# Coarser loads, deeper buffers and a new hand-written order in a sketched-attention kernel with a gated convolution

## The chip, the core and the metric

The kernel runs on one core of a Trainium2 chip. The core has five engines that run their own instruction lists in order and meet through semaphores: TensorE (PE), VectorE (DVE), ScalarE (ACT), GpSimd (POOL) and SyncE (SP, which here only issues DMAs). ACT can issue DMAs too. The metric is the device time of one execution in microseconds (us), as a median over runs.

## What is computed

For each of 4 batches and 4 heads, q, k and v are 1088 tokens of 32 numbers. A sketch phi maps a token to 64 numbers, the outer product of two projections to 8. Keys and values are summed into one 64x32 matrix per head (linear attention without a mask), each query is read against it and divided by its denominator. The heads are joined to 128 channels; a causal depthwise convolution of 5 taps gives a sigmoid gate, which multiplies a 128x128 product, and a second 128x128 product gives the output.

```python
def phi(x):
    a = np.einsum('rd,bhsd->bhsr', S1, x); b = np.einsum('rd,bhsd->bhsr', S2, x)
    return np.einsum('bhsi,bhsj->bhsij', a, b).reshape(*x.shape[:-1], r * r)
q_p, k_p = phi(q), phi(k)
kv = np.einsum('bhsf,bhsd->bhfd', k_p, v); z = np.sum(k_p, axis=2)
num = np.einsum('bhsf,bhfd->bhsd', q_p, kv)
den = np.einsum('bhsf,bhf->bhs', q_p, z)[..., None] + 1e-06
x = (num / den).transpose(0, 2, 1, 3).reshape(B, S, H * D)
gate = sigmoid(sum(conv_w[t] * xp[:, t:t + S, :] for t in range(5)))   # xp: x with 4 zeros in front
out = (gate * (x @ w_val)) @ w_out
```

## The kernel before

A batch lies in SBUF as 128 rows: 4 heads by 32 blocks m, with 34 tokens t in a row. Every piece of work is a small step function (`s_kt`, `s_kp` and so on), and the string `ORDER` lists all steps by hand: `kt20` is step kt of batch 2, part 0, and the digits behind a colon say which of seven PSUM banks it uses. Nothing else orders the work: each engine runs its share of the list in that order and holds everything behind an instruction that waits.

The steps of one batch, with the engine that does each:

- `ld`: DMA loads on SP, constants and weights on ACT. k and q of batch 0 come in two parts, of the other batches whole (544 KB); v comes as four loads of 128 KB by j (8 tokens of each row for 32 partitions) and two of 16 KB for the last two tokens (`v_lo`).
- K side: `kt` transposes k on DVE, `kp` projects on PE, `ke` copies to `kab` on ACT, `kd` (DVE) and `ko` (POOL) form the outer products `phik` (the table `KD` says how many chunks DVE takes), `kv` sums them against v on PE.
- `pz`, `pv`, `pm`, `pe`: the sums become weights for the query side (DVE, ACT, PE, ACT).
- Q side, in halves U and groups g: `qt` transposes q (DVE), `qp` projects (PE), `qc` copies (ACT), `qm`, `qr`, `qn` make the denominator, its sum and reciprocal (`qr`, DVE) and the scaled first factor `an` (DVE or POOL by `QM_POOL` and `QN_POOL`), `qo` the outer product `phi` (DVE or POOL by `QO_POOL`), `qx` transposes it on PE, `qe` copies it to `phiT` (ACT, or DVE where `ON_DVE` names it), `nm` is the numerator (PE) and `xe` copies it to the gate's input.
- Gate: `hl` copies the halo (POOL), `gt` is the convolution as 5 diagonal matmuls (PE), `sg` the sigmoid (ACT), `vl` the value product (PE), `gv` gate times value (DVE), `om` the output product (PE), `oe` the copy to SBUF, `so` the store (SP, or ACT by `ST_ACT`).
- `cn`: constants (masks and identities on POOL, wq on DVE, weight casts on POOL); `zz` and `cn06` are dummy matmuls on zeros. `cn10` in the order runs the mask step a second time.

Most tiles have two buffers by batch or half, `phi` and `phiT` three. A DMA uses one of eight completion semaphores in turn, and its issue waits until the DMA that last used this semaphore has landed. All matmuls but the transposes go through the helper `mm` and so stand under L138 in the profile; copies by ACT through `copy` under L220, by DVE under L218.

Of the kernel before, what the change touches and what calls it, by code (L numbers as in the profile page):

```python
# [9 lines left out]
BF16 = mybir.dt.bfloat16  # L10
AX = mybir.AxisListType
# [13 lines left out]


ORDER = """
cn08 ld00 cn00 ld02 cn06:01 ld03 ld06 cn09 cn10 cn01 cn07 ld07
cn02 kt00 zz07:2 ld12 ld04 kt01 ld05 ld16 kp00:2 kp01:3 ke00 zz04:0
kd00 ko00 ke01 ld01 ko01 ld17 kd01 kv00 zz01:0 ld22 kv01 ld14  # L30
kt10 ld26 zz03:0 pv00 pz00 qt00 kp10:4 pm00:5 qt01 ke10 kp11:6 pe00
ld27 ko10 kd10 qp00:0 ke11 ld32 kd11 ko11 qp01:1 ld24 qc00 ld36
kv10 qm00 qc01 cn05 qr00 kv11 qm01 qn00 qr01 cn03:2 zz02:3 pv10
qo01 cn04 pz10 qo00 ld37 pm10:3 kt20 qx00:5 ld34 qn01 qx01:4 pe10
qo02 qe00 qo03 kp20:6 qe01 nm00:0 qt10 qx02:2 ke20 qx03:3 nm01:5 qe02
kp21:1 ko20 qe03 nm02:4 kd20 qp10:2 ke21 xe01 kd21 ko21 xe02 qp11:3
qc10 xe00 nm03:6 kv20 qm10 qc11 qr10 hl00 xe03 kv21 qm11 qn10
qr11 gt00:54 qo11 pv20 pz20 kt30 vl00:1 pm20:0 sg00 sg01 gt01:26 pe20
qn11 gv00 kp30:5 qo10 qt20 sg03 sg02 kp31:4 ke30 vl02:0 ko30 qx10:1
qo12 ke31 vl03:6 qp20:2 qe10 ko31 gv02 kd31 gv03 nm10:4 qx12:3 kd30  # L40
qc20 om01:0 qx11:1 xe10 qp21:6 oe01 qm20 qr20 qe12 kv30 so02 qo13
so03 qt30 kv31 qe11 qn20 qc21 qx13:4 pz30 qo20 nm11:5 qo21 pv30
nm12:0 qe13 vl01:3 pm30:1 xe11 nm13:6 gv01 qm21 qx21:4 xe12 qx20:2 pe30
hl10 qr21 om00:50 qe21 qp30:3 xe13 qn21 qe20 oe00 qo22 nm21:1 gt11:46
qc30 xe21 so00 vl12:2 qm30 qo23 nm20:0 sg12 vl13:5 qr30 qx22:1 so01
xe20 qp31:4 sg13 gv12 qe22 qn30 qx23:0 gv13 gt10:62 qc31 qo30 qo31
qe23 nm22:1 qm31 sg10 vl11:5 qr31 vl10:3 nm23:0 sg11 om11:4 qx30:6 xe23
hl20 gv10 qx31:2 oe11 qn31 gv11 gt20:03 qe30 qo33 xe22 so12 qe31
om10:45 sg20 so13 vl20:1 nm30:6 sg21 qo32 qx33:0 gv20 xe30 nm31:2 vl21:3
oe10 qe33 gt21:16 gv21 xe31 so10 nm33:0 sg22 qx32:4 hl30 om20:52 xe33  # L50
sg23 so11 vl22:3 qe32 vl23:1 gt30:60 oe20 gv22 nm32:4 so20 gv23 sg30
vl31:2 vl30:5 xe32 sg31 om21:3 so21 gv30 gt31:16 oe21 gv31 vl32:4 om30:05
sg32 so22 vl33:3 sg33 gv32 oe30 so23 gv33 om31:2 so30 so31 oe31
so32 so33
# [4 lines left out]
def kernel(  # L59
# [34 lines left out]
    v_in = [st(f"v_in{b}", [P, H, 8 * D]) for b in range(B)]  # L94
    v_lo = [st(f"v_lo{b}", [64, H, D]) for b in range(B)]
    kT = [st(f"kT{i}", [P, NT * M]) for i in range(2)]
    qT = [st(f"qT{i}", [P, NT, M]) for i in range(2)]
    kab = [st(f"kab{i}", [P, 2, 5, 32]) for i in range(2)]
    phik = [st(f"phik{i}", [P, 5, H, 64]) for i in range(2)]
    zm = [st(f"zm{i}", [P, 32]) for i in range(2)]  # L100
    kvf = [st(f"kvf{i}", [P, 2, 64]) for i in range(2)]
    kvb = [st(f"kvb{i}", [P, P], BF16) for i in range(2)]
    wq = [st(f"wq{i}", [P, 96]) for i in range(2)]
    abc = [st(f"abc{i}", [P, 3, 5 * 32]) for i in range(2)]
    pden = [st(f"pden{i}", [P, 20, 9]) for i in range(2)]
    den = [st(f"den{i}", [P, 20]) for i in range(2)]
    an = [st(f"an{i}", [P, 20, 8]) for i in range(2)]
    phi = [st(f"phi{i}", [P, 12, 64], BF16) for i in range(3)]
    phiT = [st(f"phiT{i}", [P, 2, 320], BF16) for i in range(3)]
    xe = [st(f"xe{i}", [P, 4 + NT, M], BF16) for i in range(2)]  # L110
    gate = [st(f"gate{i}", [P, 320], BF16) for i in range(4)]
    gv = [st(f"gv{i}", [P, 576], BF16) for i in range(2)]
# [14 lines left out]
    wo_f = st("wo_f", [P, 2, P])  # L127
# [26 lines left out]
    def s_const(b, i):  # L154
# [13 lines left out]
        elif i == 9:  # L168
            make_identity(nc, ident32)
            make_identity(nc, ident)  # L170
            for t in range(2):
                nc.gpsimd.memset(pden[t], 1e-6)
                nc.gpsimd.memset(xe[t][:, 0:4, 0:1], 0.0)
                nc.gpsimd.memset(kvb[t], 0.0)
        elif i == 1:
            nc.vector.transpose(sT[:, 0, :], s1raw)
            nc.vector.transpose(sT[:, 1, :], s2raw)
            nc.vector.tensor_mul(
# [4 lines left out]
        elif i == 2:  # L183
            nc.vector.tensor_copy(out=wq[1][:, 0:64], in_=wq[0][:, 0:64])
# [7 lines left out]
            )  # L192
        elif i == 3:
# [7 lines left out]
        elif i == 5:  # L201
            nc.gpsimd.tensor_copy(out=wv, in_=wv_f)
            nc.gpsimd.tensor_copy(out=wo, in_=wo_f)
        elif i == 6:
            for t in range(9):
                mm(bank("cn", b, i, t % 2), zero[:, 0:P], zero)
        elif i == 7:
            nc.scalar.activation(out=gate[0][:, 0:1], in_=zero[:, 0:1], func=ACT.Sigmoid)
        elif i == 8:
            nc.vector.memset(zero, 0.0)  # L210
# [11 lines left out]
    def s_ld(b, i):  # L222
        if i == 0:
            nc.scalar.dma_start(out=s1raw, in_=bc(S1, 0, [16, r, D]))  # L224
            nc.scalar.dma_start(out=s2raw, in_=bc(S2, 0, [16, r, D]))
        elif i == 1:
# [306 lines left out]
```

## Time and profile before

| | us |
|---|---|
| timed runs | 58.89, 61.43, 59.87; median 59.87 |
| profiled execution, device time | 58.25 |
| its span | 56.2 |
| PE busy in the span | 46.1 (82%) |
| DVE busy | 37.5 (67%) |
| ACT busy | 32.7 (58%) |
| POOL busy | 31.8 (57%) |
| DMA: bytes moved, mean rate | 9.32 MB, 166 GB/s |

The span runs from the first to the last instruction of the profile; the device time has some 2 us around it. Busy time of PE counts matmuls from start to modelled end, so that a chain of dependent small matmuls looks full. A row of a group gives line, engine, operation, output and input tiles, shapes, count, then busy time, mean duration in ns, and the idle time of the engine just before. The slices cut the span in 40 parts of 1.4 us, one digit each in tenths. The chain of waits follows the work that ended last back to what released it.

### The profile page before, as it was taken

To read this page: it belongs to the slowest core of one execution; us is meant where nothing else is said; L and a number is where in the kernel's file an instruction comes from. 1 tells how busy PE (TensorE), PEld (TensorE's weight loads), DVE (VectorE), ACT (ScalarE), POOL (GpSimd) and SP (SyncE) were. 2 spreads that over 40 slices of the span, in tenths; PEclk is the share of its full clock that TensorE was granted. 3 is DMA by queue.
4 is the path that set the end of the run, shared out by engine and by line. 5 is a ranking of instruction groups with operands and counts; after the bars stand their busy time and mean duration, and the time that the engine had idled before them with its cause. 6 is when DMAs were issued, how large, how long until landed. Compare 5 with 4: busy or idle time off the path is not lost.

```text
span 56.2 us, 2707 instructions
## 1 busy us (share of the span) xinstructions
PE 46.1 (82%) x1131; PEld 34.0 (61%) x1131; DVE 37.5 (67%) x89; ACT 32.7 (58%) x90; POOL 31.8 (57%) x61
## 2 busy tenths in 40 slices
PE   1999989999999788999914999999999999972000
PEld 0334374758984486886804998888979776640000
DVE  1013948959898779888676889696899679850000
ACT  0450014015647999755830698799999997894000
POOL 4894008703679948979960599969799940000000
PEclk9999999999999999999999999999999999999955
DMA  0597999976679999999528302400331247566870
GB/s 0 146 332 208 183 308 381 249 127 146 116 248 421 274 222 323 317 275 169 106 44 251 142 0 47 146 18 12 89 77 44 55 96 184 137 156 156 216 213 0
DMA packets 7254, 9.32 MB, mean 166 GB/s; under 512 B 2245, under 2 KB 4938, under 8 KB 7242
## 3 DMA queue, kind: packets, MB, share of 16 engines
q1 hardware_dynamic: 6256, 8.52, 57.1%
q10 hardware_dynamic: 986, 0.63, 4.7%
q8 instruction: 9, 0.15, 1.2%
q14 instruction: 3, 0.02, 0.1%
HBM read 6.92 MB, written 2.23 MB: 163 GB/s over the span
## 4 chain that ended last, share of the span: by engine, by line
PE 44%; DMA 25%; DVE 8%; issue 6%; ACT 4%; ACTq 2%; SPq 1%; DVEq 0%
PE ring L138 33%; DMA q_in<-in_q_dram 11%; DMA wv_f<-in_moe_w_val_dram 8%; DMA s2raw<-in_S_dram 6%; PE ring L408 5%; PE kv L138 5%; DVE qT L340 2%; DVE kT L256 2%; ACTq L224 1%; ACT osb L220 1%; ACT phiT L220 1%; ACTq L479 1%; DVE xe L218 1%; SPq L235 1%; ACT kab L272 1%
## 5 line engine op out<-in xcount | busy, mean ns | idle before, releaser
L278 POOL TENSOR_TENSOR phik<-kab 128x256 f32<-128x256 f32 (+3 forms) x8 | 9.5, 1182 | 10.4 <-ACT kab L272 10.4
L394 POOL TENSOR_TENSOR phi<-an,abc 128x512 bf16<-128x512 f32 (+1 forms) x11 | 13.0, 1189 | 0.5
L138 PE MATMUL ring<-zero 128*128 128x512 bf16 x26 | 8.7, 482 | 1.3 <-DVE zero L210 1.3
L272 ACT COPY kab<-ring 128x256 f32<-128x256 f32 (+1 forms) x8 | 3.2, 402 | 8.6 <-PE ring L138 8.3
L138 PE MATMUL ring<-wq,kT 128*64 128x64 f32 x144 | 6.0, 226 | 2.6 <-issue 2.0
L220 ACT COPY phiT<-ring 128x512 bf16<-128x512 bf16 (+1 forms) x13 | 7.7, 617 | 0.3 <-ACT phiT L220 0.2
L138 PEld LDWEIGHTS ring<-wq,kT 128*64 128x64 f32 x144 | 5.0, 137 | 4.2 <-issue 2.1
L453 DVE TENSOR_TENSOR gv<-gate,ring 128x256 bf16<-128x256 bf16 x16 | 6.3, 434 | 1.7 <-PE ring L138 1.2
L138 PE MATMUL ring<-wq,qT 128*64 128x96 f32 x144 | 7.2, 248 | 0.2 <-DVE qT L340 0.2
L408 PE MATMUL ring<-ident,phi 128*64 128x128 bf16 (+1 forms) x144 | 6.7, 219 | 0.2 <-POOL phi L394 0.2
L138 PEld LDWEIGHTS ring<-wq,qT 128*64 128x64 f32 x144 | 6.2, 137 | 0.5 <-DVE qT L340 0.4
L138 PE MATMUL ring<-xe,diag 64*64 64x256 bf16 (+1 forms) x160 | 6.5, 280 | 0.1
L278 DVE TENSOR_TENSOR phik<-ring,kab 128x768 f32<-128x768 f32 (+1 forms) x7 | 5.7, 833 | 1.2 <-ACT kab L272 1.2
L442 ACT ACTIVATE gate<-ring 128x256 bf16<-128x256 f32 (+1 forms) x16 | 5.6, 399 | 1.1 <-PE ring L138 1.0
L340 DVE STREAM_TRANSPOSE qT<-q_in 128x1088 f32<-128x1088 f32 (+2 forms) x5 | 5.2, 1063 | 1.2 <-DMA q_in<-in_q_dram 1.2
L138 PEld LDWEIGHTS <-zero 128*128 128x128 bf16 x26 | 2.8, 119 | 5.2 <-issue 2.9
L408 PEld LDWEIGHTS <-phi 128*64 128x64 bf16 (+1 forms) x144 | 5.2, 109 | 1.0 <-POOL phi L394 0.3
L256 DVE STREAM_TRANSPOSE kT<-k_in 128x1024 f32<-128x1024 f32 (+1 forms) x5 | 5.0, 1020 | 0.3 <-DMA k_in<-in_k_dram 0.3
L138 PE MATMUL kv<-phik,v_in 128*32 128x64 f32 x256 | 5.2, 222 | 0.0
L138 PEld LDWEIGHTS kv<-phik,v_in 128*32 128x32 f32 x256 | 4.4, 110 | 1.1 <-DVE phik L278 0.4
L363 ACT COPY abc<-ring 128x480 f32<-128x480 f32 (+1 forms) x8 | 4.2, 519 | 1.4 <-PE ring L138 1.1
L138 PEld LDWEIGHTS <-diag 64*64 64x64 bf16 x160 | 4.2, 106 | 1.2 <-issue 0.4
(62 smaller groups left out, 75.5 us busy)
## 6 DMA issues: line engine op xcount, KB each, us to landing
v_in<-in_v_dram SPq DMA_DIRECT2D x16, 128.0 KB, 5.2
out_dram<-osb SPq DMA_DIRECT2D x13, 128.0 KB, 2.4
k_in<-in_k_dram SPq DMA_DIRECT2D x3, 544.0 KB, 4.5
q_in<-in_q_dram SPq DMA_DIRECT2D x3, 544.0 KB, 6.2
out_dram<-osb ACTq DMA_DIRECT2D x3, 128.0 KB, 2.6
k_in<-in_k_dram SPq DMA_DIRECT2D x1, 288.0 KB, 3.5
q_in<-in_q_dram SPq DMA_DIRECT2D x1, 288.0 KB, 5.0
k_in<-in_k_dram SPq DMA_DIRECT2D x1, 256.0 KB, 2.9
```

The costliest lines, as they stand in the source:

```text
L138: nc.tensor.matmul(o, lhsT=lhsT, rhs=rhs, start=start, stop=stop, skip_group_check=True, **kw)
L218: nc.vector.tensor_copy(out=out, in_=in_)
L220: nc.scalar.copy(out=out, in_=in_)
L256: nc.vector.transpose(o, i_)
L272: nc.scalar.copy(out=kab[u][:, :, 0 : 4 + u, :], in_=kab_view(b, u))
L278: eng.tensor_mul(phik[u][:, c0:c1].rearrange("p c h (i j) -> p (c h) i j", i=r), bc(a_, 3, [P, n, r, r]), bc(b_, 2, [P, n, r, r]),)
L340: nc.vector.transpose(flat(qT[b % 2][:, t0 : t0 + n, :]), q_in[b][:, t0 * D : (t0 + n) * D])
L363: nc.scalar.copy(out=abc[U][:, k0:3, 0 : 32 * ns], in_=bank("qp", b, U)[:, 32 * ns * k0 : 96 * ns].rearrange("p (k x) -> p k x", k=3 - k0),)
L394: (nc.gpsimd if pool else nc.vector).tensor_mul(phi[(4 * b + g) % 3][:, 0:n, :].rearrange("p c (i j) -> p c i j", i=r), bc(an[U][:, lo : l ...
L408: nc.tensor.transpose(o[64 * (h % 2) : 64 * (h % 2) + 64, h // 2, c * P : c * P + n], phi[(4 * b + g) % 3][:n, 4 * c + h, :], ident[:n, :n],)
L442: nc.scalar.activation(out=gate[g][:, 0:n], in_=bank("gt", b, g // 2, g % 2)[:, 0:n], func=ACT.Sigmoid)
L453: nc.vector.tensor_mul(o[:, 0:512].rearrange("p (c w m j) -> p w j c m", c=4, w=2, m=M)[:, w], view(gate[g]), view(vl))
```

## The change

It rewrites the loads, the depth of the buffers, the split of work between engines and the whole order. A short description speaks of 30 loads instead of 46; by the code it is 31 load DMAs instead of 41.

- v is loaded by j with the last tokens in it: four loads per batch, of 8, 8, 9 and 9 tokens (`KEYS`), and `v_lo` goes. k's transposes follow the same split. The fifth chunk of the K side now stands in partitions 64 to 127.
- w_out is loaded once; the two half-swapped copies are made by POOL in the cast. The weights are loaded by SP after k of batch 2, and not by ACT.
- k of a batch is loaded before q of the batch before it, as in the old order (there too k and q are whole from batch 1 on); s2raw and half of v of batch 0 are on SP, s1raw and two loads of v on ACT.
- `wq` is made by POOL (`cn013`, copies in `cn011`); the second run of the masks goes.
- `kab`, `phik`, `abc`, `phi`, `phiT` and `gv` have four buffers, `kT`, `qT` and `xe` three, and the small ones one per batch.
- From batch 1 on both halves' denominators are summed and inverted in one instruction each (`qr`, `qi`).
- `KD`, `QM_POOL`, `QN_POOL`, `QO_POOL` and `ON_DVE` move work; the last output bank goes to two banks and is copied in halves by DVE (`oe31`) and ACT (`oe33`).

```diff
+KEYS = [(0, 8), (8, 8), (16, 9), (25, 9)]
 ORDER = """
...
+cn08 ls00 cn00 lk00 cn06:01 ls01 cn07 lk01 cn05 lv00 lv03 lv01
+cn09 lk10 cn01 lv02 kt00 lq01 lq00 cn02 zz05:2 cn010 cn013 lv10
+kt01 cn011 lv12 lv11 kp00:2 lv13 kp01:3 ke00 zz05:0 kd00 ko00 ke01
+kd01 lk20 ko01 kv00 lw00 kt10 lw01 kv01 qt01 lw02 kp11:4 pv00
+lq10 pz00 qt00 pm00:5 lv20 ke11 kp10:6 pe00 lv22 kd11 ko11 ke10
+qp00:0 lv21 ko10 qp01:1 kd10 qc00 zz03:2 kt20 lv23 qm00 cn012 lk30
+cn03:2 kv10 lq20 qc01 qr00 cn04 lv30 qm01 kp20:3 qi00 qr01 lv32
+qn00 kp21:5 qi01 lv31 qo00 qo01 kv11 lv33 ke21 qt10 ke20 lq30
+zz01:0 qn01 qx01:4 pv10 pz10 qo02 qo03 qx00:6 pm10:2 qe01 qe00 qx03:0
+pe10 nm01:3 ko21 kt30 qx02:1 qe03 qp11:4 xe01 qe02 nm00:6 ko20 nm03:2
+qp10:0 kd20 kd21 xe03 qc11 kp31:3 xe00 qt20 qc10 gt00:12 ke31 qm11
+ko31 vl01:4 qm10 sg00 vl00:5 kv20 qr10 sg01 qi10 kv21 gv01 qn11
+gv00 qn10 nm02:6 pz20 pv20 kp30:1 qo12 qo10 xe02 pm20:2 ke30 kd31
+om00:45 pe20 qx10:6 ko30 qx12:0 oe02 oe00 qp21:3 qe10 so04 qe12 so00
...
+om21:6 so20 sg30 gv31 gt31:13 oe21 gv30 vl32:0 so22 sg32 om30:54 sg33
+vl33:6 so23 gv32 oe30 gv33 oe32 so30 so31 om31:21 oe31 oe33 so34
+so33 so32
 """.split()
...
+    v_in = st("v_in", [P, B * H, 9 * D])
+    kT = [st(f"kT{i}", [P, 9 * 4 * M]) for i in range(3)]
+    kab = [st(f"kab{i}", [P, 2, 5, 32]) for i in range(4)]
...
+    def s_lv(b, j):
+        t0, n = KEYS[j]
+        queue("lv", b, j).dma_start(
+            out=v_in[32 * j : 32 * j + 32, H * b : H * b + H, 0 : n * D],
+            in_=v[b].rearrange("h (m t) d -> m h (t d)", m=M)[:, :, t0 * D : (t0 + n) * D],
+        )
+    def s_kt(b, u):
+        o = kT[b % 3].rearrange("p (c j m) -> p j c m", c=9, m=M)
+        for x in (u,) if b == 0 else (0, 1):
+            t0, n = KEYS[2 * x]
+            nc.vector.transpose(
+                o[:, 2 * x : 2 * x + 2, 0:n],
+                k_in[b][:, t0 * D : (t0 + 2 * n) * D].rearrange("p (j c d) -> p j c d", j=2, d=D),
             )
...
     def s_qr(b, U):
-        n = 4 * (5 - U)
-        nc.vector.tensor_reduce(out=den[U][:, 0:n], in_=pden[U][:, 0:n, :], axis=AX.X, op=ALU.add)
-        nc.vector.reciprocal(den[U][:, 0:n], den[U][:, 0:n])
+        x = rows(U) if b == 0 else slice(0, 36)
+        nc.vector.tensor_reduce(out=den[b % 2][:, x], in_=pden[b % 2][:, x, :], axis=AX.X, op=ALU.add)
+    def s_qi(b, U):
+        x = rows(U) if b == 0 else slice(0, 36)
+        nc.vector.reciprocal(den[b % 2][:, x], den[b % 2][:, x])
...
+    def s_oe(b, i):
+        if i == 2:
+            copy("oe", b, i, osb_lo[b], bank("om", b, 0, 1)[0:64, 0:P])
+            return
+        U = i % 2
+        o = osb[2 * b + U].rearrange("p c e -> p (c e)")
+        if last(b, U):
+            copy("oe", b, i, o[:, 256 * (i // 2) : 256 * (i // 2) + 256], bank("om", b, U, i // 2)[:, 0:256])
+        else:
+            copy("oe", b, i, o, bank("om", b, U))
...
-    KD = [[3, 2], [3, 3], [2, 2], [3, 0]]
-    QM_POOL = {(1, 1), (2, 1)}
-    QN_POOL = {(0, 0), (0, 1), (1, 0), (1, 1), (2, 0), (2, 1), (3, 0), (3, 1)}
-    QO_POOL = {(0, 1), (0, 2), (1, 0), (1, 1), (1, 3), (2, 0), (2, 2), (2, 3), (3, 1), (3, 2), (3, 3)}
+    KD = [[2, 3], [2, 5], [0, 3], [1, 2]]
+    QM_POOL = {(0, 0), (0, 1), (1, 1), (3, 1)}
+    QN_POOL = {(0, 0), (0, 1), (1, 0), (1, 1), (2, 0), (3, 1)}
+    QO_POOL = {(0, 1), (0, 2), (1, 1), (1, 2), (1, 3), (2, 2), (2, 3), (3, 0), (3, 1), (3, 2), (3, 3)}
     ON_DVE = {
-        ('oe', 0, 0), ('qe', 3, 1), ('qe', 3, 2), ('qe', 3, 3), ('xe', 0, 0), ('xe', 1, 3),
-        ('xe', 2, 2), ('xe', 3, 2), ('xe', 3, 3),
+        ('oe', 0, 2), ('oe', 1, 2), ('oe', 2, 2), ('oe', 3, 1), ('oe', 3, 2), ('qe', 0, 0),
+        ('qe', 1, 0), ('qe', 1, 2), ('qe', 2, 1), ('qe', 2, 2), ('qe', 2, 3), ('qe', 3, 0),
+        ('qe', 3, 1), ('qe', 3, 2), ('qe', 3, 3), ('xe', 1, 3), ('xe', 3, 0), ('xe', 3, 2),
+        ('xe', 3, 3),
     }
-    ST_ACT = {(0, 3), (3, 0), (3, 2)}
+    ON_ACT = {
+        ('ls', 0, 0), ('lv', 0, 2), ('lv', 0, 3), ('so', 0, 0), ('so', 2, 4), ('so', 3, 0),
+        ('so', 3, 2), ('so', 3, 3),
+    }
```

## The prediction

> **What bounds the kernel now.** I read the page's slices first, then the windows of seven microseconds, the chain of waits, and last the timeline around the chain's breaks. Slices (each 1.4 us):
>
> ```profile
> PE   1999989999999788999914999999999999972000
> ...
> DMA  0597999976679999999528302400331247566870
> GB/s 0 146 332 208 183 308 381 249 127 146 116 248 421 274 222 323 317 275 169 106 44 251 142 0 47 146 18 12 89 77 44 55 96 184 137 156 156 216 213 0
> ```
>
> Until 29 us loads and compute run side by side, later there are only stores. The DMA row is near full, yet bytes per slice fall from 381 to 116 GB/s between 11 and 15 us and to 44 at 28 us: the queue is held up there. PE has one dip, at 28 to 30 us. The chain of waits names both:
>
> ```profile
> 9.42 4.29 DMA wv_f<-in_moe_w_val_dram
> 13.71 0.02 issue
> 13.73 0.31 SPq L247
> ...
> 14.08 0.43 SPq L235
> ...
> 14.56 6.20 DMA q_in<-in_q_dram
> ...
> 28.31 1.99 issue
> ```
>
> A load of v's last tokens (L247) could not be issued before the weight wv had landed, and k and q of the next batches stood behind it on SP. The 1.99 us at 28.31 lie inside kp31, in the middle of one row of like matmuls: PE waits there for nothing that the profile shows. The windows give the late stage (us, then busy and count of PE, PEld, DVE, ACT, POOL):
>
> ```profile
> 35.00:42.00 7.00, 6.95 (x167) 5.77 (x165) 5.64 (x18) 6.51 (x19) 5.95 (x9) 1.00 0.28 70
> 42.00:49.00 7.00, 6.94 (x178) 5.41 (x176) 5.84 (x19) 6.57 (x18) 3.59 (x6) 1.00 0.43 102
> ```
>
> PE is always in a matmul, ACT has 0.9 us spare in 14, DVE 2.5, POOL 4.5. The end, from the timeline:
>
> ```profile
> 51.04 0.59 ACT L220 COPY osb<-ring 128x512 f32<-128x512 f32 x1 [0.55 <-PE ring L138]
> 51.65 0.55 ACTq L479 DMA_DIRECT2D out_dram<-osb  x1
> 52.19 0.55 SPq L484 DMA_DIRECT2D out_dram<-osb_lo  x1
> 52.83 0.56 SPq L479 DMA_DIRECT2D out_dram<-osb  x1
> ```
>
> The last copy ends at 51.63, but its second store leaves SP only at 52.83.
>
> **The sum's base.** The profiled execution took 58.25 us: span 56.2, 2.05 around it. The three timed runs have a median of 59.87, 2.8% more, so I scale the result by 59.87/58.25 = 1.028.
>
> **Loads.** A load takes the completion slot of the one eight places before it, and its issue waits for that landing (SP's waits on k_in, v_in and wv_f show it). Eight v_lo loads of 16 KB and two of W go, and W goes behind k of batch 2. In the new list the load eight places before k of batch 2 is one of v of batch 0, so nothing small holds it. Bytes up to and with k of batch 2 are 32+6x544 KB = 3.38 MB. The seven slices up to 9.8 us moved 1807x1.405 = 2.54 MB, 301 GB/s from 1.4 us on; at that pace k of batch 2 is in at 1.4+11.2+0.8 (slack for landing, my estimate) = 13.4 us, against 18.5 now (kT starts at 18.56 on its landing). Up to q of batch 2 it is 5.74 MB: 21.3 us at that pace; it was 28.47 in the trace, where qT waits 0.87 us for it. These are the two ends; I take 24, a pace of 260, nearer the undisturbed slices, since the long holds go. The loads are worth nothing by themselves: they only let DVE's later transposes start. The weights are the other side: cw_in, wv and wo now stand on SP behind k of batch 2. PE waits for cw_in in cn03 with kv10 queued behind, POOL for wv and wo with qm01 behind. By the pace taken they land at 14 to 16 us, when both engines come to them; as late as 18.5 they would cost 2 us, which the range holds. Deeper buffers (kab, phik, abc and others) I cost at nothing: the one wait for a buffer that the profile names, kab on phik, is 0.3 us.
>
> **The start.** POOL drops the second copy of the masks (two memsets and four selects, 1.24 us at 3.74 to 4.98) and takes more memsets instead (+0.9 us by the rows of 0.25, 0.21 and 0.12 us); it then makes wq itself (a 128x64 product: 0.22 on DVE, under 0.41 on POOL by its 128x128 row). That is past s2raw's landing (5.04 now; it is now second on SP, so 4.7 to 5.1). What decides is PE: 14 warm-up matmuls stand ahead of kp00 instead of 16, two of 0.21 us: 7.00 becomes 6.5.
>
> **From there to the 602nd matmul.** The gap at 28.31 is after 602 of 1131 matmuls. In the new order the 602nd is the end of om00, and next comes qx10, which needs an of batch 1. POOL decides when: it casts wo when the weights are in (cast over at 16.35 now; W is later on the queue but the queue is faster: I keep 16.3), then qm01 0.46, qn00 0.46, qo01 1.51, qn01 0.41, qo02 1.07, ko21 1.07, ko20 1.96 (between the rows of 768 and 1280), qm11 0.46, ko31 1.51, qn11 0.41, qn10 0.46 = 9.8, with eleven gaps of 0.05 10.3: 26.6. DVE's qo10 (0.67) and the semaphores bring qx10 to 27.5. DVE must fit kt30, qt20 and qr10 into the same stretch. It comes to kt20 at 14.8: kd11 ends at 15.61 now, 0.5 goes with the start and 0.3 with three dummies less before qp00. The rows from kt20 to qt20 sum to 8.3 us, so it stands at qt20 at 23.1 and waits there up to a microsecond at my landing time, beside POOL's chain. So the point comes at 27.5 instead of 28.3: -0.8.
>
> **The gap.** -2.0 if it goes, 0 if it stays, +2 if a second one comes. The nearest row is the page's queue of instructions: nine packets, 0.15 MB, 16 KB each; one of them starts at 27.75 us, just before the gap, while the DMA row is full. PE's list has three matmuls less of 1131, so a fetch falls at about the same place, but with the loads ahead it falls into an emptier queue. I take -2.0. The Trainium skill ("Runtime: NRT & Kernel Launch", section "Instruction fetch mechanics") says that the instructions come in 16 KiB blocks and that crossing a block boundary is mostly hidden. By that rule the gap is something else, which no run here shows, and may stay: the sum would be 2.0 us longer.
>
> **The late stage.** Copies move from ACT to DVE: phiT from 3 to 10 there (0.414 and 0.478 a copy instead of 0.594 and 0.694). By rows: DVE +3.0 phiT, -0.4 xe, +0.8 osb_lo, -0.3 osb, -0.9 (den and its reciprocal for both halves at once, 0.51 and 0.38 by the slope of the rows), -0.5 wq and kT; the moved qm and qn and the shares of phik cancel: +1.7 on 41.6. ACT: -4.3 phiT, -0.8 osb_lo, +0.6 the rest = -4.5 on 38.2, and five DMA issues (8.83 to 11.46). POOL: +1.2 on 33.3. ACT's 93% gives way to DVE: its rows from qo10 to the end make 21.0 us, times 0.90 (busy 37.5 to sum 41.6) 19, against the 20.6 that the last 529 matmuls took (30.30 to 50.86). So DVE has 1.6 us to spare and PE stays the bound. Between -1.6 (the stage ends as early as DVE's rows allow) and +1.6 (as much lost by copies that DVE takes up late, with PE's next group behind each) I take +0.5, as DVE has the less room of the two now.
>
> **The end.** The last bank is copied in halves by DVE and ACT (0.41 by the slope of the osb rows instead of 0.59: -0.2) and its stores leave ACT at once and 0.6 later, not SP 1.2 later: -0.6. What covers the remaining stores is landing time (2.4). I take -0.6 in all, as so30 is ahead of them on ACT (0.55).
>
> **Sum:** 56.2-0.8-2.0+0.5-0.6 = 53.3; with 2.05 it is 55.35, times 1.028 = 56.9.
>
> **Rivals.**
> *A, the gap stays* (PE's fetch is as late as before): 55.3 span, 58.95: within 2%. For it: the same number of instructions, more bytes in flight. Against: the queue is emptier at 24 to 28 us.
> *B, slower: DVE is held in order by qt20.* k and q of later batches are now taken much earlier in DVE's list. If loads land as before, qt20 starts at 28.47 instead of 23, and qm10, qr10, gv00 and all behind it stand still. Rows from qm10 on sum to 24.3, times 0.90 = 21.9: 29.8+21.9+1 for waits = 52.7, plus 5.3 from the last matmul to the end, less 0.6: 57.4 span, 61.1. It decides from a landing of about 27 us on (27+1.3+21.9+1+4.7 = 55.9). For it: the measured 28.47. Against: the holds on L247 go.
> *C, the loads land at the fast pace and ACT's relief is felt in full* (-1.6 instead of +0.5): 51.2 span, 54.7.
> *D, the change is not what its words say:* the code has 31 loads after 41, and k and q were whole from batch 1 on before. Then only the holds matter, which the sum has; no other time follows.
>
> **The numbers.** My forecast 0.48 (alone 55.3 to 58.5), A 0.20, B 0.20, C 0.12. 2% is about what a measurement of this kernel can tell from no change; it lies at 58.7 and 61.1. The forecast gives nearly all and C all of its chance to faster (0.58), A and a rest of B 0.23 to the same, B and a second gap 0.19 to slower. From 54.5 (C) to 61.0 (part of B out) holds 8 in 10.
>
> **What would show it.** Right: no slice of GB/s under 200 before 20 us; k of batch 2 in by 15 and q of batch 2 by 25; qx10 at 27 to 28; no issue gap of PE over 1 us; DVE busier than ACT after 35 us; the last store issued within 0.7 us of the last copy. Wrong: DVE idle before qT on q_in; a gap of 2 us inside like matmuls; POOL idle before wo's cast; more gv or phiT waits on DVE late.

## The result and the profile after

The changed kernel is slower: a median of 62.45 us (61.21 to 65.12, 12 runs) against 59.43 (57.88 to 61.50, 15 runs of the kernel before beside it), ratio 1.0591 with a 95% interval of 1.0521 to 1.0660. A later set of runs on another occasion gave 1.0716 (1.0650 to 1.0783). Ratios with an interval leave disturbed executions out; medians are over all executions.

The lines below are of a second profile of the unchanged new kernel, 61.51 us with a span of 59.8, as the first one (64.55 us, span 62.8) has the same gaps, the second of them longer (4.8 us instead of 2.9). Slices of the page, 1.5 us each:

```profile
PE   1999029999639910999999999999999999982000
...
PEclk9999999999999999656999999999999999999995
DMA  0669999999999999993000016100000264896890
GB/s 0 183 157 300 211 269 379 245 259 281 357 273 229 246 345 304 214 247 118 3 11 0 0 26 156 37 5 5 16 0 0 59 145 110 197 218 155 192 238 2
```

The load queue now does what the change wants: there is no trough any more like the 127, 146 and 116 GB/s of before at 11 to 15 us, and all loads are in by 28 us. But PE, nearly full in the profile of before from 7 to 28 us, now has three dips: at 6 to 9 us (slices 5 and 6), at 15 to 18 (11 and 12) and at 21 to 24 (15 and 16). Behind the last one the granted clock falls to 6, 5 and 6 tenths. The chain of waits names the dips (start, length, what):

```profile
1.96 5.72 DMA k_in<-in_k_dram
7.67 0.02 issue
7.70 0.79 DVE kT L269
...
13.81 2.10 PE ring L142 x52
15.92 1.47 issue
17.39 0.82 PE ring L142 x3
...
20.21 0.94 PE kv L142 x45
21.15 2.64 issue
23.79 0.30 PE kv L142 x3
```

The first is the second part of k of batch 0, which lands at 7.67 us; the other two are gaps like the one of before, in which PE waits for nothing that the profile shows. PE's waits have the same three at their head:

```profile
PE kv L142 <- issue: 2.6, 1, 2.6
PE ring L142 <- DVE kT L269: 2.4, 1, 2.4
PE ring L142 <- issue: 1.5, 1, 1.5
```

PE is busy 46.1 us of the span in both profiles (the sums of the windows give 46.06 and 46.14; the new kernel has three long dummies less, and 3.4 us at half clock make up for them). So the whole difference of 3.6 us stands as idle time of PE. Two windows of the late stage (columns as in the windows of before), and then the end from the timeline:

```profile
35.00:42.00 7.00, 7.00 (x218) 6.11 (x215) 6.14 (x14) 4.31 (x13) 6.13 (x8) 1.00 0.20 47
42.00:49.00 7.00, 7.00 (x181) 5.78 (x181) 6.32 (x19) 6.21 (x18) 5.47 (x7) 1.00 0.19 45
```

```profile
53.50 2.34 SPq L517 DMA_DIRECT2D out_dram<-osb  x2
...
54.43 0.37 ACT L233 COPY osb<-ring 128x256 f32<-128x256 f32 x1 [0.62 <-PE ring L142]
54.83 1.29 ACTq L517 DMA_DIRECT2D out_dram<-osb  x2
55.94 0.58 SPq L513 DMA_DIRECT2D out_dram<-osb_lo  x1
```

DVE is now the busier helper, as foreseen, and PE has no slack there, as before.

### The profile page after: what moved, and what is told of

It is laid out like the page before. It is cut to its first block, busy times and chain, and to the rows that moved or that the text cites. A ratio compares the mean times of both kernels' runs of the same rounds, so it can differ in the third digit from the quotient of the medians.

```text
span 62.8 us, 2665 instructions
## 1 busy us (share of the span) xinstructions
PE 47.1 (75%) x1128; PEld 35.9 (57%) x1128; DVE 39.0 (62%) x89; ACT 29.2 (46%) x82; POOL 32.6 (52%) x63
## 4 chain that ended last, share of the span: by engine, by line
PE 65%; DMA 10%; issue 10%; ACT 2%; DVE 2%; SPq 2%; ACTq 1%
PE ring L142 43%; PE kv L142 10%; DMA k_in<-in_k_dram 10%; PE ring L429 9%; PE ring L341 2%; ACT osb L233 2%; DVE kT L269 1%; SPq L240 1%; ACTq L517 1%; ACT gate L464 1%; DVE xe L231 1%; SPq L247 1%; PE ring L205 0%
## 5 line engine op out<-in xcount | busy, mean ns | idle before, releaser
L292 POOL TENSOR_TENSOR phik<-kab 128x512 f32<-128x512 f32 (+2 forms) x7 | 9.2, 1323 | 7.9 <-ACT kab L286 7.9
L415 POOL TENSOR_TENSOR phi<-an,abc 128x512 bf16<-128x512 f32 (+1 forms) x11 | 12.9, 1190 | 0.2
L142 PE MATMUL kv<-phik,v_in 128*32 128x64 f32 (+1 forms) x288 | 6.9, 223 | 4.6 <-issue 4.6
L142 PE MATMUL ring<-zero 128*128 128x512 bf16 x23 | 7.2, 461 | 2.3 <-DVE zero L223 1.3
L142 PEld LDWEIGHTS kv<-phik,v_in 128*32 128x32 f32 (+1 forms) x288 | 5.3, 110 | 5.6 <-issue 5.4
L429 PE MATMUL ring<-ident,phi 128*64 128x128 bf16 (+1 forms) x144 | 7.8, 240 | 0.0
L269 DVE STREAM_TRANSPOSE kT<-k_in 128x512 f32<-128x512 f32 (+1 forms) x8 | 5.5, 720 | 2.7 <-DMA k_in<-in_k_dram 2.7
L292 DVE TENSOR_TENSOR phik<-ring,kab 128x512 f32<-128x512 f32 (+3 forms) x7 | 5.7, 834 | 1.2 <-ACT kab L286 1.2
L391 POOL TENSOR_TENSOR pden<-abc 128x128 f32<-128x128 f32 (+1 forms) x4 | 1.9, 475 | 7.5 <-ACT abc L378 7.4
L336 ACT COPY kvf<-kv 128x128 f32<-128x128 f32 x4 | 1.1, 266 | 10.0 <-PE kv L142 8.5
L233 ACT CAST xe<-ring 128x256 bf16<-128x256 f32 (+1 forms) x12 | 4.6, 403 | 1.0 <-PE ring L142 1.0
```

The source lines that it names most:

```text
L142: nc.tensor.matmul(o, lhsT=lhsT, rhs=rhs, start=start, stop=stop, skip_group_check=True, **kw)
L233: nc.scalar.copy(out=out, in_=in_)
L269: nc.vector.transpose(o[:, 2 * x : 2 * x + 2, 0:n], k_in[b][:, t0 * D : (t0 + 2 * n) * D].rearrange("p (j c d) -> p j c d", j=2, d=D),)
L292: eng.tensor_mul(phik[(2 * b + u) % 4][:, c0:c1].rearrange("p c h (i j) -> p (c h) i j", i=r), bc(a_, 3, [P, n, r, r]), bc(b_, 2, [P, n, r ...
L391: (nc.gpsimd if pool else nc.vector).tensor_mul(pden[b % 2][:, rows(U), 0:8], qa(b, U, 0, pool), qa(b, U, 2, True))
L415: (nc.gpsimd if pool else nc.vector).tensor_mul(phi[g][:, 0:n, :].rearrange("p c (i j) -> p c i j", i=r), bc(a_, 3, [P, n, r, r]), bc(b_, ...
```

## A first reading: whose gap it is

The page lists a queue of instructions, with the same packets and bytes in both kernels (here that of the changed one):

```profile
q8 instruction: 9, 0.15, 1.0%
```

In the trace these are nine packets of 16 KB, and I take them to be PE's program. I counted PE's records (weight loads, matmuls and a few semaphore instructions in order of start, some 2,280; a few can be missing from a trace, which moves a count by as many) up to each gap: 1217 in the kernel before, 449 and 705 in the changed one. These differ by multiples of 256 (512 from 705 to 1217, 256 from 449 to 705). The gaps therefore look like PE at the end of one block of 256 instructions with the next one not there. The table holds this for every kernel of the study. "Pass 193 → packet for 449" gives the time at which PE passes record 193, where one block starts, and the time at which the packet starts that brings the next block, from record 449 on. The gaps are from start to start of PE's records, which makes them up to 0.3 us longer than the profile's idle time; the last column is the time at half clock before PE's last work.

| kernel | pass 193 → packet for 449 | pass 449 → for 705 | pass 705 → for 961 | pass 961 → for 1217 | gaps, us | half clock, us |
|---|---|---|---|---|---|---|
| before | 10.2 → 11.2 | 15.1 → 15.0 | 20.0 → 21.6 | 24.3 → 27.8 | 2.2 at 1217 | 0 |
| after, second profile | 11.4 → 14.9 | 17.4 → 21.2 | 23.8 → 27.0 | 30.6 → 30.8 | 1.7 at 449, 2.9 at 705 | 3.4 |
| after, first profile | 11.7 → 14.6 | 17.3 → 22.8 | 25.6 → 27.3 | 33.4 → 33.7 | 1.3 at 449, 4.8 at 705 | 6.8 |
| no_late_v | 13.3 → 16.4 | 18.7 → 20.7 | 23.2 → 24.8 | 28.8 → 29.1 | 1.3 at 449, 0.9 at 705 | 3.4 (at 8.8) |
| v0_on_sp | 10.8 → 14.3 | 16.7 → 21.5 | 24.2 → 26.2 | 32.5 → 33.0 | 1.8 at 449, 4.0 at 705 | 6.8 |
| before_no_vlo | 10.6 → 11.3 | 15.9 → 18.5 | 21.1 → 24.5 | 27.5 → 28.6 | 0.7 at 705, 2.5 at 961 | 3.4 |
| after_paced | 11.4 → 14.4 | 17.0 → 18.3 | 20.7 → 22.2 | 26.3 → 30.0 | 1.3 at 449, 1.0 at 1217 | 0 |
| after_start | 10.6 → 14.8 | 17.5 → 21.8 | 24.4 → 27.8 | 31.5 → 31.5 | 2.8 at 449, 2.0 at 705 | 6.8 |
| after_both | 11.3 → 15.9 | 18.4 → 19.7 | 23.3 → 25.8 | 28.9 → 31.4 | 2.8 at 449, 1.6 at 1217 | 3.4 |
| before_v3_later | 10.8 → 11.7 | 15.7 → 16.7 | 22.6 → 21.1 | 28.1 → 28.7 | none | 3.4 |
| after_shift | 12.2 → 14.7 | 17.2 → 19.8 | 22.5 → 27.6 | 30.3 → 31.5 | 1.1 at 449, 1.4 at 705, 2.6 at 961 | 3.4 |
| after_small_loads | 11.6 → 12.5 | 15.9 → 18.1 | 20.6 → 23.2 | 26.8 → 28.5 | none | 0 |
| after_even | 11.0 → 12.9 | 15.5 → 18.6 | 21.3 → 22.6 | 26.9 → 27.3 | 1.6 at 705, 1.1 at 1473 | 0 |
| after_even_start | 12.0 → 12.5 | 16.1 → 18.5 | 21.0 → 23.8 | 26.6 → 27.9 | 1.2 at 1473 | 0 |
| after_small_start | 9.4 → 12.3 | 14.9 → 17.8 | 20.1 → 25.1 | 27.7 → 28.9 | 1.0 at 705, 1.9 at 961 | 3.4 |
| after_even_start2 | 9.4 → 12.0 | 15.2 → 18.2 | 21.0 → 24.3 | 27.2 → 28.8 | 0.8 at 705, 0.6 at 961, 0.7 at 1217, 0.7 at 1473 | 0 |
| before_more_small | 10.6 → 11.3 | 16.0 → 19.3 | 21.8 → 24.8 | 27.3 → 28.8 | 1.3 at 705 | 3.4 |
| before_v3_look2 | 10.5 → 11.1 | 15.4 → 18.1 | 20.5 → 23.7 | 26.1 → 27.1 | 0.7 at 705, 1.6 at 961, 1.4 at 1473 | 0 |

A packet starts only after PE has passed into the block before its own, to within 0.2 us (the one exception is 1.5 us, where PE had stopped for k a few records ahead): 0 to 2 us later where the load queue is quiet or pauses, mostly 2.5 to 5.5 later where loads run back to back. Its transfer takes some 1.1 us, and PE goes on 1.2 to 1.6 us after its end in all the gaps listed. A block of matmuls without waits lasts PE 3.0 to 5.6 us. So with a quiet queue there is room, and with a full one there may be none. In after_paced and after_both the profile puts the gap at 449 down to a load of q; but the weight load that ends it waits for no semaphore, and it comes 1.5 and 1.4 us after a packet like the others.

**Theory:** the load queue, filled without pauses, makes PE's instructions late; the clock falls behind the longer gaps; the second part of k of batch 0 starts the kernel late. **Rivals:** the new order or the new shares of DVE and POOL cost the time; the gaps belong to steps, not to blocks; the start alone costs it.

## The experiments

**The kernel again (after_again, unchanged).**

> The changed kernel as it is, for a second trace. Theory 1 (starved instructions): PE's instructions come in blocks of 256 through the same DMA engines as the loads, and with a fuller load queue the blocks come late; then the gaps of PE stand at the same counts again (about 449 and 705 of PE's 2270 records), whatever their length, each ending about 1.5 us after a 16 KB packet, 2 to 6 us together; time 61 to 64 us. Theory 2 (the order itself is slower: DVE or POOL hold PE): the gaps may be gone or elsewhere and the time stays 5% above the kernel before.

61.68 us median, ratio 1.0716 (1.0650 to 1.0783); the lines of it are above.

**Fewer bytes (no_late_v).** The loads of v of batches 2 and 3 are left out, and the sums of these batches read v of batches 0 and 1.

```diff
-lq10 pz00 qt00 pm00:5 lv20 ke11 kp10:6 pe00 lv22 kd11 ko11 ke10
+lq10 pz00 qt00 pm00:5 ke11 kp10:6 pe00 kd11 ko11 ke10
...
-                   v_in[pr, H * b + h, t * D : t * D + D], phik[(2 * b + u) % 4][pr, c, h, :],
+                   v_in[pr, H * (b % 2) + h, t * D : t * D + D], phik[(2 * b + u) % 4][pr, c, h, :],
```

> v of batches 2 and 3 is not loaded (their sums read v of batches 0 and 1): eight loads, 1.11 MB, less in the queue from 13.9 us on; order and work of all engines are the same. Theory 1: at 300 GB/s the block that came at 22.8 us comes 3 to 4 us earlier, the gap at count 705 shrinks from 4.6 us to 0.5 to 1.5, the granted clock does not fall to half at 24 us, and the time falls by 4 to 6% to about that of the kernel before (ratio 0.98 to 1.02). Theory 2: within 1% of the changed kernel (ratio 1.05 to 1.07), since v of batches 2 and 3 is waited for by nobody in its trace.

61.76 us median (59.73 to 63.55), no shorter than the changed kernel's 61.68: the forecast of the time failed, and by the median the rival (within 1%) is met. The trace is of the shortest execution, span 58.0. There the gap at 705 shrinks to 0.9, as the packet for it starts 2.0 us after PE's passing instead of 3.8. The second part of k came later still (PE at record 193 at 13.3 us), and the clock fell behind that wait. So by its trace the gap follows the loads; by its time this kernel settles nothing.

**Start (v0_on_sp).** The two loads of v of batch 0 go from ACT to SP.

```diff
-        ('ls', 0, 0), ('lv', 0, 2), ('lv', 0, 3), ('so', 0, 0), ('so', 2, 4), ('so', 3, 0),
+        ('ls', 0, 0), ('so', 0, 0), ('so', 2, 4), ('so', 3, 0),
```

> The two loads of v of batch 0 that ACT issued at 1.55 and 2.11 us go to SP, behind the second part of k of batch 0. Theory 3 (the late start: kT waits 2.7 us for that part of k, kp01 at 8.84 instead of 7.52 us): kp01 at 7.2 to 7.6 and the whole kernel 1.3 to 2 us faster (ratio 1.03 to 1.04). Theory 1: kp01 earlier too, but the PE blocks come when the load queue lets them, so the gaps begin earlier and end at nearly the same time; total changes by less than 0.7 us (ratio 1.05 to 1.06).

63.41 us, ratio 1.1020 (1.0964 to 1.1076): slower than the changed kernel. kp01 starts at 6.76 us instead of 8.53. Of these 1.8 us, 0.6 are left at record 193 and 0.7 at record 449, as the packet for it starts at 14.3 instead of 14.9; the second gap, 4.0 us instead of 2.9, takes them back, and the clock is at half for 6.8. An earlier start alone is worth nothing here.

**The small loads, taken from the kernel before (before_no_vlo).** Its six 16 KB loads of v's last tokens for batches 1 to 3 are left out; the sums read those of batch 0.

```diff
-kd00 ko00 ke01 ld01 ko01 ld17 kd01 kv00 zz01:0 ld22 kv01 ld14
+kd00 ko00 ke01 ld01 ko01 kd01 kv00 zz01:0 ld22 kv01 ld14
...
-                lt = v_lo[b][:, h, :] if c == 4 else v_in[b][:, h, (4 * u + c) * D : (4 * u + c + 1) * D]
+                lt = v_lo[0][:, h, :] if c == 4 else v_in[b][:, h, (4 * u + c) * D : (4 * u + c + 1) * D]
```

> The kernel before without its six 16 KB loads of v's last two tokens in batches 1 to 3 (their sums read those of batch 0): the small loads no longer hold completion slots, so more bytes are in flight. Theory 1: k of batch 2 lands 1 to 3 us earlier (18.5 before), and PE's gap moves to an earlier block (count about 705, near 20 us) or grows; time the same or up to 4% slower. The rival that I predicted by (loads that land earlier help, the gap goes): 2 to 4% faster and no gap over 1 us.

60.30 us, ratio 1.0378 (1.0247 to 1.0509): with six loads fewer the kernel before is slower. Its slices:

```profile
PE   1999999998999869913999999999999999971000
...
PEclk9999999999999999997559999999999999999555
```

The dip has moved from 28 us to 25 (slices 18 and 19), from record 1217 to 961, and the clock falls behind it. Nothing of the order, DVE's or POOL's work is changed here. The prediction had put these holds down as the fault of the old kernel; they are what lets the instructions through.

**Loads held by buffers (after_paced), the start (after_start), both (after_both), and the kernel before with its last v later (before_v3_later).** In after_paced, k of batch 3 loads into the buffer of batch 2, and q and v of batches 2 and 3 into that of batch 1, so that a load waits for the last reader. after_start has S2 on ACT and all of v of batch 0 on SP.

```diff
-    k_in = [st(f"k_in{b}", [P, NT * D]) for b in range(B)]
-    q_in = [st(f"q_in{b}", [P, NT * D]) for b in range(B)]
-    v_in = st("v_in", [P, B * H, 9 * D])
+    k_in = [st(f"k_in{b}", [P, NT * D]) for b in range(3)]
+    k_in.append(k_in[2])
+    q_in = [st(f"q_in{b}", [P, NT * D]) for b in range(2)]
+    q_in += [q_in[1], q_in[1]]
+    v_in = [st(f"v_in{b}", [P, H, 9 * D]) for b in range(2)]
+    v_in += [v_in[1], v_in[1]]
```

```diff
-        ('ls', 0, 0), ('lv', 0, 2), ('lv', 0, 3), ('so', 0, 0), ('so', 2, 4), ('so', 3, 0),
+        ('ls', 0, 0), ('ls', 0, 1), ('so', 0, 0), ('so', 2, 4), ('so', 3, 0),
```

> The changed kernel with its late loads held back by shared buffers: k of batch 3 uses the buffer of batch 2, q and v of batches 2 and 3 use that of batch 1, and their loads stand behind the last readers of those buffers in the order. Instructions starved behind loads: the 16 KB packet that ends the gap at PE's 705th record starts by 19 us instead of 21.2, the gap there is under 1 us (2.9 to 4.8 so far), the granted clock does not fall after it, and the ratio to before is 1.00 to 1.03 (1.07 unpaced), although the loads land later than in the changed kernel. The gap at 449 stays (1 to 2 us), as the loads of k of batch 2 and of v and q of batch 1 are not held. DVE or POOL as the cause (the new order or the new shares of copies): the ratio stays at 1.06 to 1.09, or rises, as the transposes of q and k start later.

61.12 us median (before 59.15 in the same runs), span 59.2. The mechanism came as expected: the packet for 705 starts at 18.3 us, there is no gap at that record and no fall of the clock. The time did not: PE now waits for v itself, since v of batch 2 is loaded only behind the last sums of batch 1. One wait has taken the place of the other.

```profile
PE kv L145 <- DMA v_in<-in_v_dram: 2.8, 2, 1.8
```

> The changed kernel with S2 on ACT's queue behind S1 and all four v loads of batch 0 on SP, so that nothing of v stands ahead of the second part of k of batch 0. Late start as a cause of its own: that part lands at 6.5 instead of 7.7 to 8.0 us, kp01 starts at 7.0 to 7.5 instead of 8.8, and the time falls by that 1.3 us: ratio to before 1.04 to 1.06. Instructions starved behind loads: PE reaches its 449th and 705th records earlier, the packets for them are no earlier (21.2 for the second), so the gaps grow by as much and the ratio stays at 1.06 to 1.10.

62.72 us median: nothing is won, as in v0_on_sp. PE is at record 193 0.9 us earlier than in the changed kernel (10.5) and at 449 no earlier (17.5). Gaps of 2.8 and 2.0 us, half clock for 6.8.

> The two edits together: late loads paced by shared buffers, and nothing of v ahead of the second part of k of batch 0. Instructions starved behind loads: gap at the 705th record under 1 us, no fall of the granted clock, and what the start wins is kept: ratio 0.97 to 1.01. DVE or POOL as the cause: 1.05 or more.

61.62 us median against 59.15: the forecast of 0.97 to 1.01 failed. There is no gap at 705, but 2.8 us at 449, 1.6 at 1217 and the waits for v.

In before_v3_later v of batch 3 goes into the buffers of batch 2, behind the last sums of that batch:

```diff
-ld27 ko10 kd10 qp00:0 ke11 ld32 kd11 ko11 qp01:1 ld24 qc00 ld36
+ld27 ko10 kd10 qp00:0 ke11 ld32 kd11 ko11 qp01:1 ld24 qc00
...
-qc10 xe00 nm03:6 kv20 qm10 qc11 qr10 hl00 xe03 kv21 qm11 qn10
+qc10 xe00 nm03:6 kv20 qm10 qc11 qr10 hl00 xe03 kv21 ld36 ld37 ld34 qm11 qn10
...
-    v_in = [st(f"v_in{b}", [P, H, 8 * D]) for b in range(B)]
+    v_in = [st(f"v_in{b}", [P, H, 8 * D]) for b in range(3)]
```

> The kernel before with v of batch 3 in the buffers of batch 2, and its two loads (and the load of k or q behind them) issued after the last sums of batch 2 have read them, at 28 us instead of 20 to 25. Instructions starved behind loads: the packet for PE's 1217th record, which started at 27.75 us while the queue was full, starts by 25, the gap of 2.2 us goes, and the kernel is 2 to 3.5% faster than before: ratio 0.965 to 0.98. The gap as something that belongs to a place in the program and not to the queue: it stays, ratio 1.00; slower only if PE then waits for v of batch 3.

60.10 us median against 59.15: not faster. The packet for 1217 is prompt (28.1 → 28.7) and its gap is gone, but PE stood 2.4 us at record 696 for k of batch 2, and the clock fell. Another execution of it follows below.

**Steps or blocks (after_shift).** Sixteen short warm-up matmuls between kp00 and kp01, where PE waits for k.

```diff
+        elif i == 14:
+            for t in range(16):
+                mm(bank("cn", 0, 6, 0)[:, 0:32], zero[:, 0:P], zero[:, 0:32])
```

> The changed kernel with 16 more warm-up matmuls of 32 columns between kp00 and kp01, where PE waits for k anyway; the loads are as in the changed kernel. Instructions in blocks of 256: the two long gaps stay at PE's 449th and 705th record, which are now 16 matmuls earlier in the program than in the changed kernel (after 206 and 333 of its own matmuls instead of 222 and 349). Gaps that belong to a step of the program (a wait that the records do not show): they move with the step, to records 481 and 737. The time stays within 1 us of the changed kernel's.

62.78 us. The gaps are again at records 449 and 705 (221 and 347 matmuls, 16 of them the new ones), and a third one at 961; at 481 and 737 there is none. They belong to blocks of 256 instructions and not to steps.

**More loads (after_small_loads).** The changed kernel, with six loads of 16 KB added.

```diff
+        if b > 0 and j == 3:
+            for x in range(2):
+                nc.sync.dma_start(
+                    out=v_x[b][32 * x : 32 * x + 32],
+                    in_=v[b].rearrange("h (m t) d -> m h (t d)", m=M)[:, :, (32 + x) * D : (33 + x) * D],
+                )
```

> The changed kernel with six loads of 16 KB added (two behind the v loads of each of batches 1 to 3, into a tile that nobody reads), which is what the kernel before had in its place; six more DMAs, and nothing else. More bytes or more loads as the cost: slower than the changed kernel or the same, ratio to before 1.06 to 1.09. Instructions starved behind loads: a small load takes a completion slot and so leaves fewer bytes in the queue, the packets for records 449 and 705 start up to 1 us earlier, the second gap is under 2 us, and the kernel is faster with more loads: ratio 1.02 to 1.055.

60.05 us median (58.15 to 60.90) against 58.69 for the kernel before: 1.023 by the medians, without an interval. All four of its executions are shorter than the shortest of the sixteen of the changed kernel (61.21), which did not run beside them. Its slices:

```profile
PE   1999908999987997999932999999999999982000
...
PEclk9999999999999999999999999999999999999755
```

No gap at any block, and the clock stays whole to PE's last work. More loads and more bytes made the kernel faster, so the bytes are not the cost; and the order and the shares of DVE and POOL, which are those of the changed kernel, can be at most what is left. The dip at 29 us is a wait for DVE in that execution, its longest 2.1 us:

```profile
PE ring L143 <- DVE zm L336: 2.4, 2, 2.1
```

**Holds by buffers, evenly (after_even), with the start (after_even_start).** v and q in two buffers by batch parity, one buffer for k of batches 1 to 3, the weights ahead of k of batch 2; in the second kernel S2 is also on ACT and all of v of batch 0 on SP.

```diff
-kd01 lk20 ko01 kv00 lw00 kt10 lw01 kv01 qt01 lw02 kp11:4 pv00
+kd01 lw00 ko01 kv00 lw01 kt10 lw02 lk20 kv01 qt01 kp11:4 pv00
...
+    k_in = [st(f"k_in{b}", [P, NT * D]) for b in range(2)]
+    k_in += [k_in[1], k_in[1]]
+    q_in = [st(f"q_in{b}", [P, NT * D]) for b in range(2)] * 2
+    v_in = [st(f"v_in{b}", [P, H, 9 * D]) for b in range(2)] * 2
```

> The changed kernel with two buffers for v and q (batches 2 and 3 use those of 0 and 1), one for k of batches 1 to 3, the weights ahead of k of batch 2, and each late load behind the last reader of its buffer: the holds of the kernel before come back, by buffers instead of completion slots, and no load is later than its reader. Instructions starved behind loads: packets for records 449, 705 and 961 start within 2 us of PE's passing the block before, no gap over 1 us, the clock stays whole to 50 us, PE is at record 705 by 20.5 and at 1217 by 29.5 instead of 33.8, and the span is 55 to 56.5: ratio 0.975 to 1.01. The new order, DVE or POOL as the cause: 1.04 or more, with the same PE time from record 449 to 1217 as in the changed kernel (16 to 18 us).

59.58 us median against 58.69, ratio 1.0277 (0.9962 to 1.0591), span 56.9. The clock stays whole; gaps are left at 705 (1.6 us) and 1473 (1.1). PE in the timeline at the first:

```profile
19.59 0.28 PE L143 MATMUL kv<-phik,v_in 64*32 64x64 f32 x3
21.28 0.30 PE L143 MATMUL kv<-phik,v_in 64*32 64x64 f32 x3 [1.41 <-issue]
```

It breaks in the middle of a row of like matmuls, just as in the changed kernel at 21.15. From there to the last weight load of the convolution, just ahead of record 961, PE takes 5.2 us (5.2 also in no_late_v, after_paced and after_even_start, at whole clock); in the changed kernel 6.6 with 3.4 us at half clock, and in v0_on_sp 8.2 with 6.8. That is the price of the clock: 1.4 and 3.0 us.

> The same with S2 on ACT behind S1 and all v loads of batch 0 on SP, so that the second part of k of batch 0 is not behind them. If the packet for record 449 is prompt (11 to 13 us), the earlier start is kept: PE is at records 190, 449 and 705 some 0.9 us earlier than without this edit, span 54 to 55.5, ratio 0.96 to 0.995. If it is as late as in the other runs of this start (14 to 15 us), PE waits there and nothing is won: ratio as without the edit, or up to 0.02 more.

59.42 us median (57.62 to 60.04), against the same 58.69. The packet for 449 was prompt, but PE was at record 193 at 12.0, not earlier: a load of v stood behind k of batch 1, and the first sums waited to 11.5 us. The edit did not test its question.

**What is left: the start once more, with v of batch 0 ahead of k of batch 1 (after_small_start, after_even_start2).**

```diff
-cn08 ls00 cn00 lk00 cn06:01 ls01 cn07 lk01 cn05 lv00 lv03 lv01
-cn09 lk10 cn01 lv02 kt00 lq01 lq00 cn02 zz05:2 cn010 cn013 lv10
+cn08 ls00 cn00 lk00 cn06:01 ls01 cn07 lk01 cn05 lv00 lv01
+lv02 lv03 cn09 lk10 cn01 kt00 lq01 lq00 cn02 zz05:2 cn010 cn013 lv10
```

> The changed kernel with the six loads of 16 KB added, and the start of the kernel before: S2 on ACT, all of v of batch 0 on SP behind both parts of k and ahead of k of batch 1. If the late start is a cause of its own once the instructions are in time: the sums of batch 0 start at 9.7 to 10.2 instead of 11.1 us, PE is at record 190 by 10.5 (11.4 to 11.6 without), the packet for record 449 starts by 13, no gap over 1 us follows, and the time falls by about 1 us against the small loads alone: ratio to before 0.985 to 1.01. If PE catches up anyway (waits on DVE or POOL set the pace to record 961): ratio 1.02 to 1.03, as with the small loads alone.

59.33 us median, ratio 1.0334 (1.0251 to 1.0418). The kernel before had a median of 60.51 in these runs, so by the medians this kernel is the shorter one (0.98); the ratio rests on the two shortest of its eleven executions, 57.09 and 57.48. PE is at record 193 at 9.4 us, 2.2 earlier than without the edit and 0.7 earlier than in the kernel before, and by record 961 the gaps are back (1.0 us at 705 and 1.9 at 961).

> The changed kernel with holds by buffers and the same start: no load of v of batch 0 behind k of batch 1 (that order made the sums of batch 0 wait to 11.5 us in the last run). If the late start is a cause of its own: record 190 by 10.5, 705 by 19.7, span 54.5 to 56, ratio 0.965 to 1.00. If not: 1.01 to 1.03, as without this start.

59.72 us median, ratio 1.0318 (1.0118 to 1.0518), against the same executions of the kernel before (0.99 by the medians). The same start; PE waits 2.0 us for kT in four places and at four blocks. The late start is not the rest of the loss by itself: what PE wins there it waits for later, at a load or at a block.

**The kernel before with more small loads (before_more_small) and before_v3_later once more (before_v3_look2).**

```diff
-ld27 ko10 kd10 qp00:0 ke11 ld32 kd11 ko11 qp01:1 ld24 qc00 ld36
+ld27 ko10 kd10 qp00:0 ke11 ld32 kd11 ko11 qp01:1 ld24 ld28 qc00 ld36
...
+        elif i == 8:
+            for j in range(4):
+                nc.sync.dma_start(
```

> The kernel before with four more loads of 16 KB, behind q of batch 2 and ahead of v of batch 3, into tiles that nobody reads. They take four completion slots at 20 to 24 us, where its one gap arises. Instructions starved behind loads: the packet for record 1217 starts by 26 instead of 27.75 us, the gap of 2.2 us shrinks to under 1, and the kernel is faster with more loads: ratio 0.965 to 0.99. If every load costs time of its own, or the new holds make PE or DVE wait for q of batch 2: ratio 1.00 to 1.02.

58.79 us median, ratio 1.0034 (0.9972 to 1.0095): no change, where 0.965 to 0.99 was forecast. The gap at 1217 is gone, and one of 1.3 us at 705 has come, with a fall of the clock.

> A second look at the kernel before with v of batch 3 loaded after the last sums of batch 2. In the first look the gap at record 1217 was gone, but k of batch 2 landed 2.6 us later than in the profile of before (21.1 instead of 18.5), though nothing ahead of it had moved. If that is the spread from one execution to the next, it lands by 19.5 now and the span is 54 to 55.5; if it comes with the edit, it lands after 20.5 again and the span is 56.5 to 58.

59.85 us, span 58.1. PE waited 0.7 us for kT in all (2.9 in the first execution), so the late k was spread from one execution to the next; but three gaps, at 705, 961 and 1473, came instead. In this kernel the one gap can be moved and was not removed with a gain.

None of the kernels beats the kernel before by a ratio with an interval. The theory was right about where the gaps stand in every trace, and about the direction of after_small_loads and before_no_vlo. Its forecasts of the time failed in no_late_v, v0_on_sp, after_both, before_v3_later, after_even and before_more_small; in most of these another wait or another block stands where the gap was.

## Why the prediction was wrong

The forecast was 56.9 us, in a range of 54.5 to 61.0; 62.45 were measured. The prediction's own signs of being right (no issue gap of PE over 1 us) and wrong (a gap of 2 us inside like matmuls) both stand against it.

**The gap** is the step that failed. It gave back 2.0 us because "with the loads ahead it falls into an emptier queue". The identification was right (the packet of instructions that starts at 27.75 us), the direction was not: the loads moved ahead fill the queue at 11 to 24 us, where two other packets pass. Instead of −2.0 the gaps were +2.4 (4.6 us against 2.2, by the second profile), and the half clock behind them took another 1.4, a term that the sum does not have. The text priced one of the nine packets, and weighed a second gap (+2) only as a rare case. The trough of 127, 146 and 116 GB/s was read as a fault; by the trace of before the packets at 11.2 and 15.0 us passed just there, 1.0 and 0 us after PE's passing, while the one at 27.75 came 3.4 us after it. (The text has the DMA row full at 27.75; it is full up to 26.7 us, while this packet is awaited, and half busy in the packet's own slice.)

The Trainium skill ("Runtime: NRT & Kernel Launch", section "Instruction fetch mechanics") calls the crossing of a block mostly hidden. The blocks of 256 instructions are what the runs show; where the load queue is full they are hidden only in part, and the gaps of the table are 0.6 to 4.8 us long.

**Loads**: the mechanism was right, the worth was not. k of batch 2 is in at 16.4 us (its transpose starts on its landing) instead of the 13.4 and 15 of the text, and 18.56 before: SP stood 2.2 us for the landing of the second part of k of batch 0 and issued k of batch 2 at 9.80. DVE never waits for q of batch 2. Deeper buffers at nothing: no run tested them alone. The weights came late, POOL's casts are over at 18.44 instead of 16.3, but PE's waits name neither the weights nor these casts.

**The start** was costed at kp00 alone. That came at 5.79, earlier than the 6.5 of the text. But kp01 needs the second part of k, which stands behind s2raw on SP and runs beside two loads of v from ACT: it starts at 8.53 instead of 7.52. −0.5 became +1.2 (record 193 at 11.4 against 10.2). A step's second half has its own load.

**From there to the 602nd matmul** (−0.8, by POOL's chain): POOL decided nothing. The 603rd matmul starts at 33.9 us instead of 27.5, behind the gaps. PE was nearly full from 7.5 us on in the kernel before (6.81, 6.39 and 6.77 us of each 7) and its work is the same in both; without gaps it could only have been earlier by what the start gives.

**The late stage** (+0.5) and **the end** (−0.6): from the end of the gap at record 1217 to the end of the span the kernel before took 25.9 us (30.3 to 56.2), the changed one from the same record, without a gap there, 25.9 (33.9 to 59.8). Together −0.1 was predicted and 0.0 measured, but that is luck, as each was wrong. The last copy is over at 54.8 and the span ends 5.0 later, against 4.6 before (51.63 to 56.2): the end is +0.4 instead of −0.6, since SP is held in its issues (2.34 us for two) until 55.84 and the last store leaves only then. The stretch up to the last copy is 0.4 shorter instead of 0.5 longer. DVE +1.8 us (predicted +1.7), POOL +0.7 (+1.2), ACT −3.5 (−4.5).

**The sum** for the second profile against that of before, by PE's records: +1.2 at 193, +2.3 behind the gap at 449, +3.8 behind that at 705, +6.2 at 961 (1.4 of it the clock; the new order also has heavier work in this block and lighter in the next two), +3.6 at 1217, where the kernel before has its gap, and +3.6 at the end. The start (+1.2), the gaps (+2.4) and the clock (+1.4) make 5.0; the 1.4 that came back are, by difference, PE's stretches up to record 1217 outside of these, and no run takes them apart.

**The rivals**: B had the right sign and the wrong cause: DVE was not held by q (its qT of batch 2 starts at 28.24 with no wait). A (the gap stays) had the right reason, more bytes in flight, and underrated it. C did not come: its pace would have had k of batch 2 in at 13.4. D held that only the holds matter; after_small_loads bears that out, with the sign turned: the holds help.

What stays open: with the loads held the kernel stands at 1.03 of the kernel before by the three ratios with an interval (one of which, that of after_even, reaches down to 0.996), and at 0.98 to 1.02 by the medians of the five kernels. Whether something of the order or the shares still costs time is not settled by that. In the profile of after_even the 0.7 us of span are the start (+0.8) and gaps of 2.7 instead of 2.2, less small gains; but the shortest executions of the kernel before (57.05 to 57.66 us, by set of runs) are 0.6 to 1.2 us shorter than its profiled one, and where they save it isn't in any trace here. When PE asks for a block, and what each engine of the DMA does with its packet behind loads, was not seen either, only when the packet starts.

## What to carry to other kernels

Count the records of the full engine up to a gap that waits for nothing; where gaps stand at multiples of 256 apart, look at the instruction queue's packets, and price a fuller load queue by them before the gain of earlier data is booked. Loads that nobody waits for should be held behind the reader whose buffer they take, not sent as early as they can go, and not so late that their own reader waits (after_paced). Where one engine is nearly full, as PE was, a change that removes none of its work can only win in its gaps.

## What the runs showed of the hardware

- PE's gaps stand at blocks of 256 instructions; the packet of 16 KB for a block starts only when the block before has started, 0 to 2 us later in a quiet queue and mostly 2.5 to 5.5 in a full one, and PE goes on 1.2 to 1.6 us after its end.
- Six 16 KB loads that nobody reads made the changed kernel faster (1.02 by the medians instead of 1.05 and 1.07), and taking six such loads away made the kernel before slower (1.0378).
- The granted clock fell to 0.5 for 3.4 or 6.8 us behind gaps and waits of 1.9 to 4.8 us, once behind one of 1.3; it did not behind 2.2 us in the kernel before and in after_small_loads. It cost 1.4 and 3.0 us.
- Executions of the kernel before differ by 8% (57.05 to 61.77 us in the runs beside the experiments), and the time goes with the granted clock (correlation −0.59 over 53 executions).
